# Moving the late 128x128 transposes of a fused attention and ReGLU kernel from TensorE to the DMA crossbar

## The chip, the cores and the metric

One core of a Trainium2 chip. The metric is the device time of one execution in microseconds (us), lower is better. "TensorE" is the matmul engine (PE in the profile), "DVE" VectorE, "ACT" ScalarE, "POOL" GpSimd, "SP" the engine that here only issues DMAs. PSUM is the memory, in banks, that the matmuls write. A DMA "lands" when its data has arrived; the times to landing below count from its issue. "Crossbar" stands here for the path of a DMA transpose. A ratio below is the mean time of one kernel's fast runs over that of the other's fast runs of the same rounds, so it isn't quite the ratio of the medians quoted beside it. It comes with a 95% interval.

## The reference

Eight batches (B = 8) of x, 8 heads x 512 x 64, and of a state, 8 heads x 32 x 64. Two attentions without projections, then a gated feed-forward over all 544 rows of each batch:

```
scores  = x @ state^T / 8          a  = softmax(scores)    xread = a @ state      (512 rows)
scores2 = state @ x^T / 8          a2 = softmax(scores2)   sread = a2 @ x         ( 32 rows, "recurrent read")
rows    = concat(xread, sread)     # to (8*544, 512)
out     = (relu(rows @ w_gate) * (rows @ w_val)) @ w_out   # 512 -> 1536 -> 512
```

## The kernel before

The first part of the kernel is a hand-placed program up to slice 27. The part that matters here is a loop over "slices": slice g is one block of 128 hidden columns of one batch (12 to a batch), four 512-column gate/value matmuls, plus four 512-column matmuls of the output projection of an earlier batch. Other work is hung onto slices with `at(batch, block, ...)`, slice = 12 * batch + block. The loop starts with slice 28.

```python
def state_T(g):                       # states of two batches, four transposes into one PSUM bank
    ps = held["st", g] = bank("stT_ps").bitcast(BF16)[:, 0:512]
    for i in range(4):
        nc.tensor.transpose(ps..., st_b[:, g % 3, i]..., id128)
def sr_T(b, eng):                     # recurrent read of batch b, one transpose and its copy
    ps = bank("srT_ps").bitcast(BF16)[:, 0:128]
    nc.tensor.transpose(ps, held["sn", b]..., id128)
    copy[eng](out=br[:, :, b]..., in_=ps...)
def x_trans_dma(b):  nc.sync.dma_start_transpose(out=xT[b]..., in_=xb[b]...)     # already on the crossbar
def att_aT_dma(b):   nc.sync.dma_start_transpose(out=ANS[b]..., in_=a_sn[b]...)  # already on the crossbar
def att_scale(b, jp):  # DVE: a_sn = e_sn * rc, both inputs in SBUF
def x_next(b):   # POOL converts xf to bf16 (xb), then x_trans_dma(b)
def x_pad(b):    # POOL copies xb to xa, for the recurrent reads
...
at(2, 6, x_dma, 4, (nc.sync,))                 # 1 MB load of x of batch 4
at(2, 8, state_prep, 4, B)
for b in range(3, B):
    s = b - 1
    for i, jf in enumerate((4, 5) if b == 3 else (3, 5)):  at(s, jf, att_half, b, i)
    for part, jf in enumerate((7, 10)):        at(s, jf, u_block, b, part)   # three weight products
    if b + 1 < B:  at(s, 9, x_next, b + 1); at(s, 9, x_pad, b + 1)
    if b + 2 < B:  at(s, 10, x_dma, b + 2, (nc.sync,))
for b in range(B):
    s, jf = {0: (2, 3), 1: (2, 4), 2: (2, 7), 3: (2, 10)}.get(b, (b - 1, 10))
    if b > 1:  at(s, jf, sr, b)
    at(s, jf + (2 if b in (2, 3) else 1), sr_T, b, "act")
```

Every engine works in its own order. Gate, value and weight products share six PSUM banks in turn, two banks for each product; a bank is free when ACT and DVE have read it.

The softmax here doesn't subtract the row's maximum and nothing guards it: scores larger than these inputs give would overflow.

## Time and profile before

| | before |
|---|---|
| time, median of 3 runs | 223.18 us (223.1 to 223.2) |
| span of the profile | 222.2 us |
| time of the profiled run itself | 223.98 us |
| TensorE busy / DVE / ACT / POOL | 97% / 59% / 56% / 22% |
| chain that ended last | 94% TensorE |

The lines are in the prediction.

The changed kernel:

```profile
5.50:11.10 5.60, 4.95 (x82) 3.00 (x80) 3.73 (x9) 2.77 (x4) 4.29 (x7) 1.00 1.51 174
```

### The profile page before, as it was taken

How to read it: one execution, taken by the hardware profiler on the slowest of the kernel's cores; microseconds unless marked ns; L12 is line 12 of the kernel's file. 1: busy time of each engine (PE TensorE's matmuls, PEld its weight loads, DVE VectorE, ACT ScalarE, POOL GpSimd, SP SyncE). 2: the span in 40 equal slices, each digit the busy share in tenths (PEclk: the TensorE clock that was granted, in tenths of full speed). 3: DMA queues.
4: the chain of work that ended last, by engine and by line, in shares of the span. 5: the costliest groups of instructions: out<-in, count | busy, mean ns of one | idle time of the engine just before them, and what ended most of it. 6: DMA issues, size and time to landing. Idle time of an engine off the chain costs nothing.

```text
span 222.2 us, 4878 instructions
## 1 busy us (share of the span) xinstructions
PE 216.5 (97%) x1971; PEld 106.6 (48%) x1971; DVE 130.0 (59%) x229; ACT 124.7 (56%) x238; POOL 48.9 (22%) x54
## 2 busy tenths in 40 slices
PE   7799999999999999999999999999999999999994
PEld 3455454444544444444444444445444445666544
DVE  3587888965795558664777368646874433222100
ACT  5389888475667555574466456645655444322222
POOL 8766935360002425015000700000000000000000
PEclk9699999999999999999999999999999999999999
DMA  6999999171055772771169114511311112222132
GB/s 153 172 194 197 198 242 278 44 191 48 0 133 201 133 247 66 160 249 49 51 134 275 62 52 93 99 47 50 94 50 47 49 47 50 50 47 71 73 95 95
DMA packets 38007, 25.48 MB, mean 115 GB/s; under 512 B 19200, under 2 KB 33408, under 8 KB 37984
## 3 DMA queue, kind: packets, MB, share of 16 engines
q1 hardware_dynamic: 25120, 16.95, 27.4%
q0 software_dynamic: 11968, 7.47, 21.8%
q10 hardware_dynamic: 896, 0.75, 1.2%
q8 instruction: 15, 0.25, 0.4%
q14 instruction: 8, 0.07, 0.1%
HBM read 18.35 MB, written 8.91 MB: 123 GB/s over the span
## 4 chain that ended last, share of the span: by engine, by line
PE 94%; DMA 4%; ACT 0%; issue 0%; POOL 0%; DVE 0%; DVEq 0%; POOLq 0%
PE o_ps L353 39%; PE gv_ps L316 38%; PE gv_ps L333 5%; PE up L291 4%; DMA xb<-in_x_dram 3%; PE sc_ps L200 2%; PE upc L291 2%; PE sr_ps L264 1%; PE xT_ps L186 1%; PE warm_ps L435 1%; DMA out_dram<-o_sb 1%; PE aT_ps L235 1%; PE xT_ps L173 0%; PE stT_ps L129 0%; ACT o_sb L361 0%
## 5 line engine op out<-in xcount | busy, mean ns | idle before, releaser
L353 PE MATMUL o_ps<-wo_sb,h_sb 128*128 128x512 bf16 x372 | 94.8, 379 | 0.0
L316 PE MATMUL gv_ps<-ans,U 128*128 128x512 bf16 x384 | 94.4, 379 | 0.0
L344 DVE TENSOR_TENSOR h_sb<-gv_ps,g_sb 128x512 bf16<-128x512 f32 x96 | 64.9, 689 | 43.3 <-ACT g_sb L340 42.1
L340 ACT ACTIVATE g_sb<-gv_ps 128x512 bf16<-128x512 f32 (+1 forms) x108 | 62.9, 588 | 45.9 <-PE gv_ps L316 35.0
L316 PEld LDWEIGHTS <-U 128*128 128x128 bf16 x384 | 36.0, 98 | 40.7 <-issue 0.4
L353 PEld LDWEIGHTS <-h_sb 128*128 128x128 bf16 x372 | 35.2, 98 | 39.7 <-issue 1.6
L361 ACT COPY o_sb<-o_ps 128x512 f32<-128x512 f32 x31 | 18.3, 590 | 17.4 <-PE o_ps L353 17.4
L301 ACT CAST U<-up 128x512 bf16<-128x512 f32 x36 | 18.9, 593 | 12.1 <-PE up L291 12.0
L142 POOL CAST xb<-xf 128x1024 bf16<-128x1024 f32 x10 | 10.6, 1086 | 66.9 <-DMA xf<-in_x_dram 66.9
L301 DVE CAST U<-up 128x512 bf16<-128x512 f32 x36 | 22.7, 684 | 4.2 <-PE up L291 3.7
L213 DVE TENSOR_REDUCE cs<-e_sn 128x16 f32<-128x512 bf16 x16 | 10.9, 683 | 8.3 <-ACT e_sn L207 8.3
L256 POOL COPY xa<-xb 128x2048 bf16<-128x2048 bf16 (+1 forms) x9 | 15.2, 1707 | 1.6 <-issue 1.3
L344 DVE TENSOR_TENSOR hs_sb<-gv_ps,g_sb 128x256 bf16<-128x256 f32 x12 | 5.1, 425 | 15.3 <-PE gv_ps L333 10.8
L207 ACT ACTIVATE e_sn<-sc_ps 128x512 bf16<-128x512 f32 x16 | 9.6, 600 | 7.7 <-PE sc_ps L200 7.7
L219 DVE TENSOR_TENSOR a_sn<-e_sn,rc 128x512 bf16<-128x512 bf16 x16 | 11.7, 734 | 0.4
L291 PEld LDWEIGHTS <-stT 64*32 64x32 bf16 x512 | 5.9, 90 | 9.5 <-issue 8.1
L311 ACT CAST U<-upc 128x512 bf16<-128x512 f32 (+1 forms) x21 | 10.1, 566 | 0.5 <-PE upc L291 0.4
L200 PEld LDWEIGHTS <-xT 128*128 128x128 bf16 x128 | 6.0, 100 | 4.2 <-DVE xT L177 0.9
L291 PE MATMUL up<-wg_sb,stT 64*32 64x512 bf16 x144 | 7.5, 382 | 0.0
L435 PE MATMUL warm_ps<-hs_sb 128*128 128x512 bf16 x15 | 6.3, 535 | 1.2 <-DVE hs_sb L399 1.2
L291 PE MATMUL up<-wv_sb,stT 64*32 64x512 bf16 x144 | 7.2, 380 | 0.0
L333 PE MATMUL gv_ps<-br,wg_sb 128*128 128x256 bf16 x48 | 7.2, 273 | 0.0
(63 smaller groups left out, 123.8 us busy)
## 6 DMA issues: line engine op xcount, KB each, us to landing
out_dram<-o_sb SPq DMA_DIRECT2D x27, 256.0 KB, 2.4
xf<-in_x_dram SPq DMA_DIRECT2D x4, 1024.0 KB, 6.4
wo_sb<-in_moe_w_out_dram POOLq DMA_DIRECT2D x2, 768.0 KB, 13.4
wg_sb<-in_moe_w_gate_dram POOLq DMA_DIRECT2D x5, 256.0 KB, 9.6
wv_sb<-in_moe_w_val_dram POOLq DMA_DIRECT2D x5, 256.0 KB, 10.0
out_dram<-o_sb SPq DMA_DIRECT2D x9, 128.0 KB, 2.3
xf<-in_x_dram POOLq DMA_DIRECT2D x1, 1024.0 KB, 15.0
xb<-in_x_dram POOLq DMA_DIRECT2D x3, 256.0 KB, 6.4
```

The lines of the kernel that those rows point to most:

```text
L142: copy[eng](out=xb[b][:, :, hs].rearrange("p c h d -> p h c d"), in_=xf[b][:, hs])
L213: nc.vector.reduce_sum(out=cs, in_=e_v, axis=AX.X)
L219: {"dve": nc.vector, "pool": nc.gpsimd}[eng].tensor_tensor(out=by_pair(a_sn[b], jp).rearrange("p r (j n) -> p r j n", n=Ns), in0=e_v, in1= ...
L256: nc.gpsimd.tensor_copy(out=v[:, hs:hs + src.shape[1]], in_=src)
L291: nc.tensor.matmul(dst[parity][32 * j:32 * j + 32], stT[r:r + 64, b, j, 32 * parity:32 * parity + 32], wsb[r:r + 64, j, lo:lo + n], start= ...
L301: copy[eng](out=U[b][:, w, kc, lo:lo + 512], in_=held["u", b, w, lo][kc])
L316: nc.tensor.matmul(ps[w], U[b][:, w, kc, f0:f0 + 128], ANS[b][:, kc].rearrange("p c t -> p (c t)"), start=(kc == 0), stop=(kc == NK - 1))
L333: nc.tensor.matmul(ps[w][:, 0:nt], wsb[:, j, f0:f0 + 128], br[:, j].rearrange("p b n -> p (b n)"), start=(j == 0), stop=(j == NJ - 1))
L340: nc.scalar.activation(out=g_sb[:, 0:n], in_=ps[0][:, 0:n], func=AF.Relu)
L344: nc.vector.tensor_tensor(out=dst, in0=ps[1][:, 0:n], in1=held["g", b, jf][:, 0:n], op=ALU.mult)
L353: nc.tensor.matmul(held["o", b, tsub], src[:, jf, tsub * 128:(tsub + 1) * 128], wo_sb[:, jf], start=(jf == 0), stop=(jf == NF - 1))
L361: copy[eng](out=o_sb, in_=held["o", b, tsub])
```

## The change

It takes the sixteen transposes of the loop from TensorE and issues them as DMA transposes on the SP queue, into the still unused `hs_sb`; ACT's copies read them there, six slices after (five after the issue, for the reads). It also leaves two output stores of batch 6 whole. Its core:

```diff
+    def state_T_dma(g):
+        t = held["st", g] = spare[:, 512 * g:512 * g + 512]...
+        nc.sync.dma_start_transpose(out=t, in_=st_b[:, g % 3]...)
...
-    def sr_T(b, eng):
-        ps = bank("srT_ps").bitcast(BF16)[:, 0:128]
-        nc.tensor.transpose(ps, held["sn", b]..., id128)
+    def sr_T_dma(b):
+        t = held["snT", b] = spare[:, 2048 + 128 * b:2048 + 128 * b + 128]...
+        nc.sync.dma_start_transpose(out=t, in_=held["sn", b]...)
+    def sr_out(b, eng):
         copy[eng](out=br[:, :, b]..., in_=ps...)
...
-        n = 2 if b == B - 2 else 1
+        n = 2 if b == B - 2 and tsub < 2 else 1
...
-    at(2, 8, state_prep, 4, B)
+    for g in (2, 3):
+        at(2, 2 + g, state_T_dma, g)
+        at(2, 8 + g, state_out_dma, g, "act")
...
-        at(s, jf + (2 if b in (2, 3) else 1), sr_T, b, "act")
+        at(s, jf + 1, sr_T_dma, b)
+        at(s, jf + 6, sr_out, b, "act")
```

More of the change, by code (lines that the diff above doesn't have):

```diff
@@ L72 @@
     hs_sb = const.tile([128, NF, B * Ns], BF16, name="hs_sb")
-    warm = hs_sb.rearrange("p f n -> p (f n)")[:, 0:512]
+    spare = hs_sb.rearrange("p f n -> p (f n)")
+    warm = spare[:, 0:512]
     tiny = const.tile([128, 1], FP32, name="tiny")
@@ L130, in state_T, with state_out_dma @@
                                 st_b[:, g % 3, i].rearrange("p h d -> p (h d)"), id128)
+    def state_T_dma(g):
+        t = held["st", g] = spare[:, 512 * g:512 * g + 512].rearrange("p (i t) -> p i t", i=4)
+        nc.sync.dma_start_transpose(out=t, in_=st_b[:, g % 3].rearrange("p i h d -> p (i h d)"))
+    def state_out_dma(g, eng):
+        copy[eng](out=stT[:, 2 * g:2 * g + 2].rearrange("p b j m -> p (b j m)").rearrange("p (q i m) -> p q i m", i=4, m=8),
+                  in_=held["st", g].rearrange("p i (q m) -> p q i m", m=8))
     def state_out(g, eng):
@@ L273, in sr_norm @@
         nc.vector.tensor_tensor(out=sn, in0=ps[:, :, 0:D], in1=rr.to_broadcast([128, 2, D]), op=ALU.mult)
-    def sr_T(b, eng):
-        ps = bank("srT_ps").bitcast(BF16)[:, 0:128]
-        nc.tensor.transpose(ps, held["sn", b].rearrange("p r d -> p (r d)"), id128)
+    def sr_T_dma(b):
+        t = held["snT", b] = spare[:, 2048 + 128 * b:2048 + 128 * b + 128].rearrange("p (o t) -> p o t", o=1)
+        nc.sync.dma_start_transpose(out=t, in_=held["sn", b].rearrange("p r d -> p (r d)"))
+    def sr_out(b, eng):
+        ps = held["snT", b].rearrange("p o t -> p (o t)")
         copy[eng](out=br[:, :, b].rearrange("p j (m i) -> p j i m", i=4), in_=ps.rearrange("p (j i m) -> p j i m", i=4, m=8))
@@ L504, in sr @@
         sr_norm(b)
-    def state_prep(lo, hi):
-        for g in range(lo // 2, hi // 2):
-            state_T(g)
-            state_out(g, "act")
     first, lag = 2 * NF + 4, 18
     at(2, 6, x_dma, 4, (nc.sync,))
-    at(2, 8, state_prep, 4, B)
+    for g in (2, 3):
+        at(2, 2 + g, state_T_dma, g)
+        at(2, 8 + g, state_out_dma, g, "act")
     for b in range(3, B):
```

## The prediction

> **What bounds the kernel now.** I read first the busy times and the 40 slices of the page, then the chain that ended last, then that chain in order of time around the removed instructions, and last the timeline of all engines there.
>
> The head of the page:
>
> ```profile
> span 222.2 us, 4878 instructions
> PE 216.5 (97%) x1971; PEld 106.6 (48%) x1971; DVE 130.0 (59%) x229; ACT 124.7 (56%) x238; POOL 48.9 (22%) x54
> PE   7799999999999999999999999999999999999994
> PEclk9699999999999999999999999999999999999999
> PE 94%; DMA 4%; ACT 0%; issue 0%; POOL 0%; DVE 0%; DVEq 0%; POOLq 0%
> ```
>
> TensorE is busy in every slice but the first two and the last, at the full clock, and 94% of the chain that ended last is TensorE. No other engine is above 59%. A busy TensorE alone proves little, since matmuls overlap; so I look at the chain in order of time, which shows whether one matmul follows the last without a hole. This is the chain in the stretch where most of the removed instructions stand (columns: start in us, length in us, what):
>
> ```profile
> 57.95 0.23 PE sc_ps L200 x8
> 58.18 0.06 PE srT_ps L277
> 58.24 0.86 PE gv_ps L316 x4
> ...
> 65.81 0.86 PE gv_ps L316 x4
> 66.68 0.45 PE stT_ps L129 x8
> 67.12 0.86 PE gv_ps L316 x4
> 67.99 0.86 PE o_ps L353 x4
> 68.85 0.06 PE srT_ps L277
> 68.91 0.86 PE gv_ps L316 x4
> ```
>
> The reader is to see that each start plus its length is the next start: 66.68 + 0.45 = 67.13, 68.85 + 0.06 = 68.91. The chain never leaves TensorE here. So the two kinds of transposes that go, L129 (states) and L277 (recurrent read), stand on the path with exactly these lengths, and what follows each of them can start that much sooner. Four 512-column matmuls take 0.86 us, 0.216 us each, though the groups list 379 ns as their duration: durations overlap, starts don't. The same holds for the transposes, so the lengths in the chain are used below and not the 219 ns of their rows.
>
> **What the Trainium skill says.** "Perfetto Trace Analysis", section "Identifying the Most-Contended Engine", says that matmul busy time is a poor measure of distance to the roofline because matmuls are pipelined. The trace agrees (379 ns against a spacing of 216), which is why I used the chain. "VectorE: DVE Perf Modes", section "The three transpose paths", gives 390 ns for a 128x128 bf16 transpose on TensorE and 1309 ns on the DMA crossbar. The first doesn't fit here: 219 ns each, and only 0.056 to 0.06 us of the path. The second can't be read off before, where only larger ones run; they land after 3.1 us (8 blocks) and 4.4 us (16 blocks). "DMA: Bandwidth & Descriptors", section "Rules for kernel authors", advises issuing a DMA early, computing, and waiting late, so that the fixed cost overlaps; the six slices are this advice. Its section "DMA Transpose (X-bar)" wants 2-byte data, an SBUF destination and one stream at a time: all transposes here are bf16, into SBUF, and all issued from SP.
>
> **The change part by part.** (1) *Removed from TensorE.* The compiled programs differ by 32 rows on TensorE, 16 weight loads and 16 transposes: 2 groups x 4 for the states of batches 4 to 7, and 8 for the recurrent reads. On the path: 0.45 us for the first 8, and 8 x about 0.057 = 0.46 us for the others (the chain shows 0.06 at 58.18, 60.20, 68.85 and 97.02; 0.45 / 8 = 0.056). Sum **0.90 us**. The weight loads lie beside matmuls and add nothing.
>
> (2) *Added to the SP queue.* Two transposes of four 128x128 blocks and eight of one block. The queue's timeline has this (start, length of the issue):
>
> ```profile
> 72.60 2.04 SPq L159 DMA_TRANSPOSE xT<-xb  x1
> ...
> 87.17 1.24 SPq L227 DMA_TRANSPOSE ans<-a_sn  x1
> ```
>
> 16 blocks take 2.04 us and 8 take 1.24, so 0.10 us a block and 0.44 fixed: an estimate of 0.84 us for a state and 0.54 for a read, 2 x 0.84 + 8 x 0.54 = 6.0 us of queue time in all. In a steady batch of 23.4 us SP issues about 2.1 (xT) + 1.0 (xf) + 1.2 (ans) + 4 x 0.34 (outputs) = 5.7 us, so 0.54 more leaves it mostly idle. Landing, by the same straight line through 3.1 and 4.4 us: about 2.5 us for four blocks and 2.0 for one. Nothing of this is on the path if the data is there when the copy asks.
>
> (3) *Is it there?* A slice is one gate/value block with its output part, about 1.73 us (2 x 0.86), more with attention in it. State transposes are issued in slices 28 and 29 (near 58 and 61 us) and read in slices 34 and 35 (from about 70 us): some 9 us for about 3.3 of issue and landing. Reads are issued one slice after they are computed and copied five slices later, 8.6 us or more. The tightest is batch 3: its sn is ready near 73.4, but in SP's order it stands behind the transpose of x for batch 4 and the next load of x, which end at 74.73 + 0.84 = 75.6; it lands near 78.1, and its copy comes after slice 40, whose matmuls start at 80.8. That leaves 3 us. So no new wait.
>
> (4) *The copies on ACT stay*, two of 588 ns and eight of 445 ns, now from SBUF. Here I looked for a crowd: slice 34 now gets a state copy and a read copy beside its three U copies. The timeline before:
>
> ```profile
> 69.38 0.60 ACT L340 ACTIVATE g_sb<-gv_ps 128x512 bf16<-128x512 f32 x1
> 71.04 1.56 ACT L301 CAST U<-up 128x512 bf16<-128x512 f32 x3 [1.06 <-PE up L291]
> 72.77 0.59 ACT L361 COPY o_sb<-o_ps 128x512 f32<-128x512 f32 x1 [0.17 <-PE o_ps L353]
> ```
>
> ACT is idle for 1.06 us just before the U copies, and the state copy stands exactly there; the read copy then delays the output copy and the next ReLU by some 0.3 us, and ACT was idle 1.13 us three slices later. A ReLU a few tenths late holds up TensorE only when the six PSUM banks run out, three pairs on, so this is hidden too.
>
> (5) *Ten fewer turns of the six PSUM banks.* Each transpose took a bank; without it the same bank is asked for one use later. This can only loosen, and there was no hole to close.
>
> (6) *Two output stores are no longer cut in halves* (batch 6): two issues of 0.34 us fewer, 20 us and more before the end. Nothing. [...]
>
> **Sum:** 223.18 - 0.90 = 222.28 us, 0.4%.
>
> **Rivals.** (a) *A transpose arrives late and ACT waits.* ACT runs in order: ReLU stops, then DVE, then TensorE for want of banks. For it: SP also runs in order and stands still for long times, 30.1 us once for the converted x (L159 waiting for L142). Against it: those waits lie before the first slice or behind loads issued early, and the smallest slack above is 3 us. A late read on every batch by 1 us past ACT's slack of about 1 us would cost up to 6 us in all, 228; I give this 2 in 100.
> (b) *SP gets too slow for the other transfers*, the attention transpose of batch 3 above all, which now has two state and one read transpose ahead of it. Before, it was issued at 62.89 when its data was ready; the three should be out by about 62. Even 2 us late, landing at 68, it is early for batch 3's first slice near 74. Nothing, or some tenths.
> (c) *TensorE's time is given back*: with it 0.9 us ahead, a later wait simply grows. For it: DVE and ACT wait for TensorE throughout, so they are close behind. Against it: they are the ones waiting (L340 for L316, 35.0 us), at 59% and 56%, and the chain has no hole outside the start and the tail. Then 223.1.
> (d) *More than the sum*: a transpose also hinders the weight loads around it. The matmuls after one take 0.86 us, as others do, so I give it no more than 0.3 us, 222.0.
>
> **Range and chances.** Centre 222.3 us from the sum. The runs of before spread by 0.1 us. Below, (d) and a little from looser banks: 221.7. Above, (c) with a tenth or two of ACT's crowding: 223.2. A gain of over 2% would need 4.5 us; all 16 transposes at their full 219 ns are 3.5 us, so it can't come from here. A loss of over 2% needs (a) in most batches.
>
> **What would show it.** Right: TensorE 16 instructions fewer, span near 221.3; in the chain, slices follow one another at 0.86 us with no srT_ps, and only half the stT_ps. ACT's copies of br and stT show no wait for a DMA. The ten transposes land in 2 to 3 us. Wrong: ACT copies of br or stT listed as waiting for hs_sb, or TensorE idle in slices 28 to 42; the state copies growing much beyond 588 ns, since they now gather their input in runs of eight elements; an output or xT issue seen behind a new transpose with someone waiting for it. If the span falls by clearly less than 0.9 us, the place where the chain leaves TensorE tells which.

## More of the kernel before

The busy times by stretch (columns: stretch, its length, busy us of PE, PEld, DVE, ACT and POOL with counts, granted TensorE clock, DMA share, GB/s), before:

```profile
5.50:11.10 5.60, 4.39 (x54) 2.68 (x51) 3.07 (x6) 2.11 (x4) 4.39 (x8) 0.70 1.50 172
```

## The result and the profile after

223.05 us, median of four runs (222.78 to 223.1), against 223.14 for the kernel before (222.9 to 223.2, four runs); ratio 0.9996, interval 0.9978 to 1.0013. The time is the same. It lies in the predicted range, but 0.75 us above its centre; nearly all of the expected 0.9 us is missing.

The profile after seems to say otherwise:

```profile
span 221.3 us, 4871 instructions
...
PE 88%; DMA 7%; DVE 1%; ACT 1%; POOL 1%; issue 1%; DVEq 0%; POOLq 0%; ACTq 0%
```

The span is exactly the 221.3 us of the prediction, by chance: the profile of before was about 1 us too long at its start (before_again, below, has 221.1). The true news is in the second line. TensorE holds 88% of the chain, 94% before, and DMA 7%, 4% before. The chain at this place before:

```profile
87.07 0.86 PE o_ps L353 x4
87.94 0.83 PE up L291 x24
88.76 0.97 PE o_ps L353 x4
```

The chain after, in order of time, shows where it leaves TensorE (L365 is the old L353, L328 the old L316, L303 the old L291; the change moved the lines):

```profile
75.72 0.45 PE gv_ps L328 x2
76.17 0.02 issue
76.19 0.61 ACT g_sb L352
76.80 0.02 issue
76.82 0.06 DVE h_sb L356
76.88 5.92 DMA hs_sb<-sn
...
82.82 0.02 ACT br L290
...
86.34 1.29 DVE h_sb L356 x2
87.63 0.04 issue
87.67 0.41 PE up L303 x7
```

The crossbar transpose of the recurrent read of batch 3 takes 5.92 us from issue to landing. ACT's copy waits for it, ACT's later work is late, so DVE's products are late, and TensorE finds no free bank for the third weight product of slice 43. The waits confirm the middle of it:

```profile
ACT br L290 <- DMA hs_sb<-sn: 2.3, 1, 2.3
```

To measure this free of the start I use four landmarks of TensorE: the first score matmul (sc_ps) of slice 28, where the two programs begin to differ; the first weight product (up) of slice 43; that of slice 46; and the first matmul of the last output piece (L382, L394 after). Starts from the timelines, in us:

| kernel | 28 to 43 | 43 to 46 | 46 to last piece | whole stretch |
|---|---|---|---|---|
| before, both profiles | 30.08 | 6.11 | 122.51 | 158.70 |
| changed | 29.46 | 6.81 | 122.30 | 158.57 |
| changed, again | 29.47 | 6.55 | 122.29 | 158.31 |

So 0.61 us is gained up to slice 43 and 0.22 after slice 46, 0.83 in all; 0.44 to 0.70 us is given back in one slice.

### The profile page after: what moved, and what is told of

Same layout as the page of the kernel before. It is cut to its first block, busy times and chain, and to the rows that moved or that the text cites. A ratio compares the mean times of both kernels' runs of the same rounds, so it can differ in the third digit from the quotient of the medians.

```text
span 221.3 us, 4871 instructions
## 1 busy us (share of the span) xinstructions
PE 216.4 (98%) x1955; PEld 105.9 (48%) x1955; DVE 129.9 (59%) x229; ACT 125.1 (57%) x238; POOL 48.6 (22%) x54
## 4 chain that ended last, share of the span: by engine, by line
PE 88%; DMA 7%; DVE 1%; ACT 1%; POOL 1%; issue 1%; DVEq 0%; POOLq 0%; ACTq 0%
PE o_ps L365 37%; PE gv_ps L328 36%; PE gv_ps L345 5%; PE up L303 4%; DMA xb<-in_x_dram 3%; DMA hs_sb<-sn 3%; PE upc L303 2%; PE sc_ps L209 1%; PE sr_ps L273 1%; DMA out_dram<-o_sb 1%; PE xT_ps L195 1%; PE aT_ps L244 1%; DVE h_sb L356 1%; ACT o_sb L373 1%; POOL xb L427 0%
## 5 line engine op out<-in xcount | busy, mean ns | idle before, releaser
L365 PE MATMUL o_ps<-wo_sb,h_sb 128*128 128x512 bf16 x372 | 94.8, 379 | 0.0
L328 PE MATMUL gv_ps<-ans,U 128*128 128x512 bf16 x384 | 94.0, 379 | 0.0
L328 PEld LDWEIGHTS <-U 128*128 128x128 bf16 x384 | 36.2, 98 | 42.2 <-issue 0.4
L365 PEld LDWEIGHTS <-h_sb 128*128 128x128 bf16 x372 | 35.2, 98 | 39.7 <-issue 1.6
L151 POOL CAST xb<-xf 128x1024 bf16<-128x1024 f32 x10 | 10.1, 1042 | 67.5 <-DMA xf<-in_x_dram 67.5
L303 PEld LDWEIGHTS <-stT 64*32 64x32 bf16 x512 | 6.0, 90 | 10.6 <-issue 9.3
L303 PE MATMUL up<-wg_sb,stT 64*32 64x512 bf16 x144 | 8.0, 382 | 0.2 <-DVE h_sb L356 0.2
L303 PE MATMUL up<-wv_sb,stT 64*32 64x512 bf16 x144 | 7.6, 380 | 0.0
L345 PE MATMUL gv_ps<-br,wv_sb 128*128 128x256 bf16 x48 | 7.2, 273 | 0.0
```

What stands on the lines that cost most here:

```text
L151: copy[eng](out=xb[b][:, :, hs].rearrange("p c h d -> p h c d"), in_=xf[b][:, hs])
L303: nc.tensor.matmul(dst[parity][32 * j:32 * j + 32], stT[r:r + 64, b, j, 32 * parity:32 * parity + 32], wsb[r:r + 64, j, lo:lo + n], start= ...
L328: nc.tensor.matmul(ps[w], U[b][:, w, kc, f0:f0 + 128], ANS[b][:, kc].rearrange("p c t -> p (c t)"), start=(kc == 0), stop=(kc == NK - 1))
L345: nc.tensor.matmul(ps[w][:, 0:nt], wsb[:, j, f0:f0 + 128], br[:, j].rearrange("p b n -> p (b n)"), start=(j == 0), stop=(j == NJ - 1))
L365: nc.tensor.matmul(held["o", b, tsub], src[:, jf, tsub * 128:(tsub + 1) * 128], wo_sb[:, jf], start=(jf == 0), stop=(jf == NF - 1))
```

## The experiments

Twelve runs in three jobs on three chips. Times of whole runs scattered more than in the first measurement: the kernel before took 222.5 to 225.5 us in the first job, with TensorE's landmark of slice 28 anywhere from 56.6 to 59.9 us in the profiles. Below, the stretch from slice 28 on decides, and the time ratio is given beside it. No ratio is as much as 2% from 1; one run of load_after (226.24 us) was slow and isn't counted.

| run | 28 to 43 | 43 to 46 | 46 to last | stretch | ratio (95% interval) |
|---|---|---|---|---|---|
| before_again | 30.08 | 6.11 | 122.51 | 158.70 | 1.0001 (0.9951, 1.005) |
| after_again | 29.47 | 6.55 | 122.29 | 158.31 | 0.9995 (0.9969, 1.002) |
| late3 | 29.47 | 6.56 | 122.29 | 158.32 | 0.998 (0.9938, 1.0022) |
| load_after | 29.47 | 6.11 | 122.29 | 157.87 | 1.0016 (0.9962, 1.007) |
| load_after_b | 29.47 | 6.61 | 122.29 | 158.37 | 0.9992 (0.997, 1.0014) |
| pool_copy3 | 29.47 | 7.51 | 122.28 | 159.26 | 1.0067 (1.0015, 1.0119) |
| load_pool | 29.47 | 7.39 | 122.28 | 159.14 | 1.0045 (1.0016, 1.0073) |
| xf4_early | 29.52 | 6.11 | 122.29 | 157.92 | 0.9978 (0.9953, 1.0002) |
| xf4_early_b | 29.56 | 6.11 | 122.29 | 157.96 | 0.9964 (0.9947, 0.9982) |
| xf4_only | 29.55 | 6.11 | 122.30 | 157.96 | 0.9974 (0.9951, 0.9996) |
| only_states | 29.63 | 6.41 | 122.51 | 158.55 | 0.9973 (0.9951, 0.9994) |
| only_reads | 29.92 | 6.55 | 122.29 | 158.76 | 0.9999 (0.9977, 1.0021) |

The first and third columns repeat to a few hundredths among variants with the same transposes on TensorE; what varies is slice 43 to 46.

**before_again**, the kernel before without an edit.

> The kernel before, unedited, as a control. Its profile on record has a span of 222.2 us and a granted clock of 0.70 between 5.5 and 11.1 us, and its profiled run took 223.98 us where its plain runs took 223.1. Theory: that profile is 0.8 us long in its first 20 us, by the clock alone; a new profile has a span near 221.4 us with a full clock in the second slice, and the matmuls of slice 28 start near 57.2 and not 58.0. If instead the span is 222.2 again at a full clock, the two profiles do differ by 0.9 us from the change. Ratio to itself 1.000 within 0.0015.

Span 221.1 us with the landmark of slice 28 at 56.72, not 57.79; the stretch 158.70 again. The old profile was long by its start alone.

**after_again**, the changed kernel without an edit.

> The changed kernel, unedited, beside the repaired ones on one chip. The stretch from the first score matmul of slice 28 (from there on the programs differ) to the first matmul of the last output piece was 158.70 us in both profiles of the kernel before, and 158.57 us in the changed kernel. Theory: this stretch repeats to 0.05 us, with 0.6 us gained before the weight products of slice 43, 0.7 lost in that slice and 0.2 gained after; and the time before slice 28 scatters by a microsecond and more, with no part in the change. Rival: the stretch scatters too, and 158.57 was chance; then it comes out anywhere from 157.8 to 159.3. Time ratio to before 0.9995 within the scatter.

Half right: the two outer columns repeat to 0.01 us, the loss of slice 43 was 0.44 this time and not 0.70, and the stretch differs by 0.26 us, not by 0.05. The next runs found why the loss varies.

**late3**, the copy of batch 3 two slices later.

```diff
-        at(s, jf + 6, sr_out, b, "act")
+        at(s, jf + (8 if b == 3 else 6), sr_out, b, "act")
```

> The changed kernel with one edit: the copy that reads the recurrent transpose of batch 3 stands eight slices after it was computed instead of six. Theory A (one late transpose gave the gain back): the transpose of batch 3 still lands about 5.9 us after its issue, but the copy no longer waits (0 us for 2.29 us), TensorE keeps its spacing through 82 to 88 us, and the time is 222.3 us, ratio to before 0.996. Rival B (the gain is returned by whatever wait is next, wherever it is): the wait goes, the time stays near 223.0, ratio 0.9985 to 1.000. Rival C (the time of a run doesn't follow TensorE's chain to a few tenths at all): no change in time either, 223.0.

The transpose still landed after 5.8 us and ACT no longer waited, but slice 43 still lost 0.45 us: theory A was not the whole cause, and rival B describes this run. (Its time ratio has too wide an interval to decide.) The timeline of this run, DVE's scaling of the scores and POOL's copy (start, length):

```profile
83.29 1.90 POOL L265 COPY xa<-xb 128x2048 bf16<-128x2048 bf16 x1
84.59 1.14 DVE L228 TENSOR_TENSOR a_sn<-e_sn,rc 128x512 bf16<-128x512 bf16 x1
```

The same two in before_again:

```profile
83.06 1.90 POOL L256 COPY xa<-xb 128x2048 bf16<-128x2048 bf16 x1
85.35 0.69 DVE L219 TENSOR_TENSOR a_sn<-e_sn,rc 128x512 bf16<-128x512 bf16 x1
```

In late3 the scaling takes 1.14 us, where it took 0.69 at this place in both profiles of the kernel before. POOL's copy ends at 85.19, the scaling at 85.73, 0.54 us after. In each of the seven runs where a POOL instruction still ran when this scaling began, the scaling ended 0.54 us after that instruction, to 0.01: durations of 0.75 (after_again), 0.93, 0.99, 1.14, 1.19, 1.43 and 2.09 us. So DVE waits for POOL's instruction. The reverse is seen in load_after: POOL's copy began 0.06 us after the scaling and took 2.39 us, not 1.90. The Trainium skill, "SBUF — State Buffer", section "Who interferes with whom", states it: a DVE instruction with two SBUF inputs contends with a GpSimd instruction that reads SBUF, and the later one blocks fully. The prediction did not look there. In the kernel before, POOL's copy ended 0.39 us (before_again) and 0.11 us (first profile) before the scaling began: the two just missed each other.

Taken over all runs, the end of this scaling accounts for the loss. In late3, load_after_b, pool_copy3 and only_states ACT doesn't wait for the transpose, and the scaling takes 0.45, 0.50, 1.39 and 0.30 us longer than 0.69: the losses are 0.45, 0.50, 1.40 and 0.30. In the four runs in which ACT waits, the scaling also starts late, by ACT's wait less about 1.6 us: 0.70 for a wait of 2.29 (the changed kernel), 0.38 for 1.97 (after_again), 0.54 for 2.13 (load_pool) and 0.20 for 1.78 (only_reads). With 0, 0.06, 0.74 and 0.24 us of blocking added, these are the losses of 0.70, 0.44, 1.28 and 0.44. Not every blocked scaling costs time: that of the first half of batch 4 took 0.97 us in the first profile of before and 1.52 in only_states, and neither run lost anything by it.

**load_after**, and **load_after_b** as a repeat: the load of x for batch 5 behind the transpose of batch 3.

```diff
-            at(s, 10, x_dma, b + 2, (nc.sync,))
+            at(s, 12 if b == 3 else 10, x_dma, b + 2, (nc.sync,))
```

> The changed kernel with one edit: the 1 MB load of x for batch 5 is issued on the SP queue after the recurrent transpose of batch 3 instead of before it; the transpose of x for batch 4 stays ahead of it. Theory A1 (the transpose of batch 3 lands late because the load is in front of it on the same queue): it lands after 2.5 to 3 us instead of 5.9, no wait at the copy, time 222.3, ratio 0.996. Rival A2 (it lands late because of the crossbar transpose of x ahead of it, or of its own one-block shape): it still lands after 5 us or more, the copy still waits about 2 us, time 223.0.

> The repaired order once more (the load of x for batch 5 after the recurrent transpose of batch 3), since its first timing was lost in the scatter of the start. Theory A1: the stretch from slice 28 to the last output piece is 157.87 us again (0.83 less than before), slice 43 keeps its 6.11 us to slice 46, and the time ratio to before comes out at 0.996 on a quiet chip. Rival: 157.87 was chance, and the loss of slice 43 is back in some runs.

The transpose landed after 2.4 us in both, and ACT didn't wait in either. So the load, not the transpose of x before it and not the one-block shape, makes it late. All profiles agree: the 42 one-block transposes issued while a 1 MB load of x was in flight landed 0.2 to 2.3 us after that load had landed, 2.7 to 6.5 us after their issue; the 46 others landed 2.2 to 2.4 us after it. But only the first run kept the whole gain: there DVE's scaling began at 87.86, 0.01 us after POOL's conversion ended at 87.85. In the repeat it began at 84.62 while the conversion ran until 85.27; it took 1.19 us and slice 43 lost 0.50. Repairing one wait left the other to chance.

**pool_copy3**, the copy of batch 3 on POOL.

```diff
-        at(s, jf + 6, sr_out, b, "act")
+        at(s, jf + 6, sr_out, b, "pool" if b == 3 else "act")
```

> The changed kernel with one edit: the copy that reads the recurrent transpose of batch 3 runs on GpSimd instead of ACT; transpose, load and their order stay. Theory A (what costs is ACT standing in its order behind the late transpose): the transpose still lands after about 5.9 us, the copy still waits for it or later, but ACT, DVE and TensorE don't, time 222.3, ratio 0.996. Rival D (the late data itself, or the traffic of load and transposes around 76 to 83 us, slows TensorE): 223.0 as in the changed kernel.

A miss: ACT didn't wait, but now POOL did (7.59 us), its conversion and copy for batch 5 came later, the scaling took 2.09 us, and slice 43 lost 1.40. This is the largest loss of all and the strongest sign of the second mechanism: the delay goes into POOL alone and comes out at TensorE.

**load_pool**, the load of batch 5 issued by POOL on its own queue.

```diff
-            at(s, 10, x_dma, b + 2, (nc.sync,))
+            at(s, 10, x_dma, b + 2, (nc.gpsimd if b == 3 else nc.sync,))
```

> The changed kernel with one edit: the load of x for batch 5 is issued by GpSimd, on its own queue, at the same place of the program, so that it is no longer ahead of the recurrent transpose of batch 3 on the SP queue but still in flight beside it. Theory Q (order in the queue delays the transpose): it lands in 2.5 to 3.5 us, ACT doesn't wait at the copy. Theory E (the DMA engines are shared, so any load of 1 MB in flight delays it): it lands after 5 us or more as in the changed kernel, and ACT waits about 2 us. In both, the load arrives about as late as before, so GpSimd's copy of x may still lie over DVE's scaling of the scores in slice 42; then slice 43 loses up to 0.5 us, stretch 158.3; if not, 157.9.

Theory E. The instructions of tile sn in this run, the transpose of batch 3 and its landing:

```profile
L286 SPq DMA_TRANSPOSE hs_sb<-sn x1: 1111/1111/1111, 77.2 to 77.2; - x1
...
DMA to landing us min/median/max: 6.5/6.5/6.5
```

With the load on another queue it landed even later, after 6.5 us; ACT waited 2.1 us. The Trainium skill, "DMA: Bandwidth & Descriptors", section "Issuing engines are not separate DMA queues", says that all queues run on the same 16 engines and interleave. This run agrees. The stretch missed its expectation: slice 43 lost 1.28, ACT's wait and a scaling of 1.43 us together.

**xf4_early**, and **xf4_early_b** as a repeat: late3 with the load of x for batch 4 issued in slice 28 instead of 30, ahead of the new transposes.

```diff
-    at(2, 6, x_dma, 4, (nc.sync,))
+    at(2, 4, x_dma, 4, (nc.sync,))
```

> The run with the copy of batch 3 two slices later, with one more edit: the load of x for batch 4 is issued in slice 28, ahead of the new transposes, instead of slice 30 behind them. In that run the copy no longer waited but slice 43 still lost 0.45 us: DVE's scaling of the scores took 1.14 us for 0.69 while GpSimd copied x, GpSimd being later relative to TensorE than before. Theory G (the new transposes hold up the SP queue by 1.15 us each, so the loads, GpSimd's conversions and its copy come later, and the copy then lies over DVE's instruction): GpSimd's conversion for batch 4 starts at least 1.3 us earlier relative to slice 28, its copy for batch 5 ends before DVE's scaling starts, that takes 0.69 us, slice 43 to 46 takes 6.11 us, stretch 157.85. Rival H (DVE is slowed by something else, or ACT's extra copy in slice 42 is what costs): slice 43 still loses 0.4 us, stretch 158.3.

> The early load of x for batch 4 with the copy of batch 3 two slices later, once more, for its time on another chip: its first timing was 0.9978 with an interval of 0.9953 to 1.0002. Theory: stretch 157.92 again to 0.05, ratio 0.9965 expected from 0.78 of 223.1 us, inside both intervals. Rival: the stretch was chance, as with the load of batch 5 moved behind the transpose (157.87, then 158.37).

Theory G, in both. The reason for the edit is SP's order. Before, the load of batch 4 follows the attention transpose at once:

```profile
62.89 1.32 SPq L227 DMA_TRANSPOSE ans<-a_sn  x1
64.32 0.52 SPq L104 DMA_DIRECT2D xf<-in_x_dram  x1
```

In the changed kernel a new transpose lies between, and takes as long to issue as the one of eight blocks before:

```profile
62.06 1.53 SPq L236 DMA_TRANSPOSE ans<-a_sn  x1
63.63 1.23 SPq L286 DMA_TRANSPOSE hs_sb<-sn  x1
64.92 0.57 SPq L105 DMA_DIRECT2D xf<-in_x_dram  x1
```

Measured from the landmark of slice 28 the load is issued 7.90 us later, 6.53 before. POOL's conversion for batch 4 begins after 14.03 us, 12.76 before, and everything behind it (the transpose of x, the load of batch 5, POOL's conversion and copy of it) is late too, while TensorE is 0.61 us early. Together that closes the gap of 0.1 to 0.4 us between POOL's copy and DVE's scaling. In the changed kernel the larger part is TensorE's lead, which alone exceeds the gap: POOL's copy for batch 5, the one that meets the scaling, ends 28.60 to 28.64 us after the landmark there (after, after_again, late3), against 28.51 and 28.24 in the two profiles of before. In only_reads it is the other way round: the copy ends after 29.05 us, and TensorE's lead is 0.16. The early load brings this copy some 5 us forward (23.3 to 24.3 us), so it takes POOL out of the way and doesn't show that SP's order alone had caused the clash. With the load early, the scaling took 0.69 us in both runs and slice 43 to 46 its 6.11.

**xf4_only**, the same one edit in the changed kernel, the copy left at six slices.

> The changed kernel with one edit alone: the load of x for batch 4 is issued in slice 28, ahead of the new transposes; the copies of the recurrent reads stay six slices after. Theory S (both losses of slice 43, ACT's wait for the late transpose of batch 3 and DVE's wait for GpSimd's copy, come from the SP queue running late): with the load early, the transpose of batch 3 is issued near 72.5 us, lands near 77.6 though a load of 1 MB is in flight, and the copy asks near 80.5: no wait. GpSimd's copy for batch 5 ends near 80.8, long before DVE's scaling near 85. Slice 43 to 46 takes 6.11 us, stretch 157.9, time ratio to before 0.9965. Rival: the six slices are too few whatever the queue does; ACT waits again and slice 43 loses 0.4 us or more, stretch 158.3.

Theory S. One moved load removes both waits (timelines of SP, POOL and DVE in this run):

```profile
72.91 1.88 SPq L286 DMA_TRANSPOSE hs_sb<-sn  x1
78.75 1.90 POOL L265 COPY xa<-xb 128x2048 bf16<-128x2048 bf16 x1
85.42 0.69 DVE L228 TENSOR_TENSOR a_sn<-e_sn,rc 128x512 bf16<-128x512 bf16 x1
```

The transpose of batch 3 is issued at 72.91 and lands after 4.6 us, still slow beside the load, but it is issued 4 us sooner than in the changed kernel (76.88); no wait of ACT is listed. POOL's copy ends 4.8 us before the scaling starts. The stretch is 157.96, the ratio 0.9974 with an interval that ends below 1: 222.61 us against 223.38. With the two runs of xf4_early (stretch 157.92 and 157.96) it is 0.74 to 0.78 us shorter than the kernel before in the stretch, a third of a per cent, and 0.35 to 0.65 shorter than the changed kernel, which wasn't timed beside it in this job. The ratio alone wouldn't show this: only_states, below, has 0.9973 in the same job with a gain of 0.15 us in the stretch. The 0.05 to 0.09 us that the first column is behind late3 are the same clash once more: POOL's conversion for batch 4 now runs beside DVE's scaling in slice 28, which takes 0.76, 0.79 and 0.78 us in the three runs, and the third weight product of slice 31 is as much longer.

**only_states** and **only_reads**, one half of the change each. In only_states, `sr_T` and its place are those of before; in only_reads, `state_prep` is.

> One half of the change: states by the crossbar, recurrent reads on TensorE as before. Sum: 0.45 us gained before slice 43, nothing after slice 46 (122.51 as before). Theory S: only one 1.2 us transpose is put ahead of the attention transpose of batch 3 and none between it and the load of x for batch 4, so GpSimd runs some 0.7 us later against TensorE (0.25 by the queue, 0.45 because TensorE is ahead); DVE's scaling had 0.39 us to spare, so it waits 0 to 0.4 us. Stretch 158.25 to 158.5. There is no read transpose that ACT could wait for. If slice 43 loses 0.6 us or more, theory S is wrong about the reads.

> The other half: recurrent reads by the crossbar, states on TensorE as before. Sum: 0.24 us gained before slice 43, 0.22 after slice 46. Theory S: one read transpose of 1.2 us stands between the attention transpose and the load of x for batch 4, so GpSimd is later by 1.2 us and more, and the transpose of batch 3 lands 5.6 us or more after its issue beside the load of batch 5; ACT waits about 2 us, slice 43 loses 0.4 to 0.7: stretch 158.6 to 158.95, no gain at all. Rival: the loss comes from the state transposes; then the stretch is 158.25.

The states alone gain 0.45 us before slice 43, as summed, and lose 0.30 there to the scaling (0.99 us), with no read to wait for: stretch 158.55, 0.05 above the expected range. The reads alone gain 0.16 and 0.22 and lose 0.44, with ACT waiting 1.8 us: 158.76, no gain at all, as theory S said. The time ratio of only_states, 0.9973, is better than its stretch (0.15 us of 223 is 0.9993); that ratio's interval of 0.9951 to 0.9994 doesn't hold it, and I put the difference down to the start, without having shown it.

## Why the prediction was right and wrong

It was right that the time stays within 2%, that TensorE's chain is the path, and that the removed transposes stand on it with their chain lengths. The range held, but not by the sum: its upper end, 223.2, came from rival (c), and the time lies just below it because most of the gain was lost again. By its steps:

- *Removed from TensorE, 0.90 us:* 0.83 measured in load_after, which lost nothing, and as the sum of the two outer columns in most others. The states' 0.45 is exact. The first four reads gave 0.16 where 0.23 was summed, the last four 0.22 as summed.
- *SP queue time, 0.54 us a read and 0.84 a state:* mis-sized. In the changed kernel's profile the issues measured 1.12 to 1.48 us for one block and 1.23 for four. The straight line through 8 and 16 blocks has no right to be drawn down to one: one, four and eight blocks all take about 1.2 us at the least.
- *Landing, 2.0 us for one block:* 2.2 to 2.4 us without a 1 MB load in flight, 2.7 to 6.5 with one, since it landed only after the load; for batch 3 in the changed kernel 5.92. The prediction named the load as what SP has to issue first, and forgot that its 1 MB still has to go through the same DMA engines.
- *"That leaves 3 us. So no new wait":* this is the step that failed. The copy of batch 3 could have started at 80.5 us, and the data came at 82.8.
- *Rival (a)* was the right one for that copy, and was given too little (its 2 in 100 was for a late read in every batch); one wait of 2.3 us cost 0.70 us at TensorE in that profile. ACT's slack, put at about 1 us, was about 1.6.
- *Rival (c), the time given back*, was nearest in size, 223.1 us, but not as put: not a TensorE that waits a little more everywhere, but one slice where ACT waited or POOL's copy and DVE's scaling met. In the changed kernel TensorE's own lead was the larger part of what made them meet. The clash between DVE and POOL was missing from the prediction altogether; ACT was checked for crowding, POOL was not.
- *"Span near 221.3"* came true for a wrong reason. The 0.9 us was subtracted from the span of a profile that was longer than its own kernel's plain runs.
- *The copies on ACT* behaved as said: 609 to 644 ns for a state (586 before) and 461 to 502 for a read (446 before).

What stays open: how often each of the two losses occurs in plain runs, since only profiled runs show it.

## What to carry to other kernels

A transfer that takes work off the busiest engine costs issue time in a queue that works in order, and what stands behind it there, above all the next load, comes later: place loads ahead of new small transfers. Take the latency of a small transfer from a moment when a large one is in flight. And where one engine is sped up, look for pairs of instructions elsewhere that only just missed each other.

## What the Trainium skill lacked or had wrong

- "VectorE: DVE Perf Modes", "The three transpose paths": 390 ns for a 128x128 bf16 transpose on TensorE; here 219 ns as listed and 0.04 to 0.06 us of TensorE's path each. It gives 1309 ns for the crossbar; here 1.1 to 1.9 us went into the issue alone, 2.2 to 2.4 us to landing with no 1 MB load in flight, and up to 6.5 us beside one.
- "DMA: Bandwidth & Descriptors", "Rules for kernel authors": the advice to issue early and wait late gives no measure of how much a load in flight lengthens a small transfer; here 2.3 us became 2.7 to 6.5, and the small transfer always landed after the load. The page also gives no issue time for a small SBUF to SBUF transpose: one, four and eight blocks took at least 1.1 to 1.2 us each on SP, sixteen 1.7 us and more.
- "SBUF — State Buffer", "Who interferes with whom": right, and decisive here. It gives no figure for this pair; the DVE instruction, 0.69 us when free, ended 0.54 us after the POOL instruction that had blocked it.
- None of the pages that I read gives a size for the scatter at the start of a one-core run: here a landmark behind an unchanged stretch of program stood between 56.6 and 59.9 us in one job.
